# Group normalisation on one core: one load over fifteen DMA engines from the GpSimd queue in place of quarter-wise statistics and transfers

## The chip, the core and the metric

The kernel runs on one core of a Trainium2 chip. The metric is the device time of one execution in microseconds (us). Before the change it is 637.84 us, the median of three runs (637.81 to 638.18).

The core has four engines that compute: TensorE (PE in the profile, with its weight loads as PEld), VectorE (DVE), ScalarE (ACT) and GpSimd (POOL). SyncE (SP) does nothing but issue transfers here. Transfers between the memory of the chip and the core's own memory of 128 partitions are carried by sixteen DMA engines. [...]

## What is computed

```python
def reference(x, g, b):          # x: (128, 1024, 32, 16) bf16
    G = 32
    xr = x.reshape(B, G, C // G, H, W)
    mu = xr.mean(axis=(2, 3, 4), keepdims=True)
    var = ((xr - mu) ** 2).mean(axis=(2, 3, 4), keepdims=True)
    xn = (xr - mu) / jnp.sqrt(var + 1e-5)
    xn = xn.reshape(B, C, H, W)
    return xn * g[None, :, None, None] + b[None, :, None, None]
```

Each sample has 32 groups of 32 channels; a group is 32 x 512 = 16384 numbers that lie next to each other. Mean and variance are those of the group, g and b belong to the channel. 134 MB are read and 134 MB written.

## The kernel before, in words

A tile is four samples with their 32 groups each, 128 groups, one to a partition: 128 rows of 16384 bf16, 32 KB a row, 4 MB a tile. There are 32 tiles (NT) and six buffers for them (XBUFS); a result is written over its own input. All the work is unrolled. The helper `chain` keeps the instructions of one engine in the order of the program text; waits between engines come from the data. Loads and stores are all issued by SP, in one order.

For a tile i:

- `L(i)` (lines 91 to 102) loads it. Tile 0 and tile 31 go in four transfers of 1 MB (a quarter of every row), the others in one of 4 MB. The first six are issued at once. After that the load of tile i + 5 is issued behind the store of tile i, and waits for the store of tile i - 1, whose buffer it takes.
- `M(i)` (155) adds the tile up on TensorE: 32 matmuls with the identity, each taking 512 columns, 8 of them into `pa` (the first quarter of the row) and 24 into `pb`.
- `R0(i)` (189) reduces `pa` on DVE to `q`, minus the first quarter's sum over 16384. `R1(i)` (192) adds `pb` to it, which gives minus the mean, and makes the `seed`, minus the square of the distance between the quarter's mean and the whole one, in small operations (198, 210).
- `Q(i)` (221) squares the tile about its first quarter's mean on ACT, in four instructions of 4096 columns, each with a sum. The squares thus need the first quarter's sum alone.
- `V(i)` (239) makes the variance on DVE (245) with the seed as correction, its root on ACT (258), the reciprocal (266), and a scale and a bias for each channel (271, 277).
- `A(i, c)` (288) writes the result of a quarter c over the tile, a DVE instruction for each channel (305). In the last tile two channels of each quarter go to ACT (298).
- `S(i, lo, hi)` (315) stores. The last two tiles go in quarters as they are done, the others whole.

The loop runs, for every i: Q(i), M(i+1), R0(i+1), V(i), then A(i) with R1(i+1) in the middle of it, the store, and the load of tile i + 5. So on DVE the first reduction of the next tile stands ahead of V(i), and on ACT the root of tile i stands ahead of the squares of tile i + 1.

g and b are loaded once as [32, 32] each from the ACT queue, and spread to the 128 partitions by a matmul (`GB`, 141).

Of the kernel before, what the change touches and what calls it, by code (L numbers as in the profile page):

```python
# [8 lines left out]
ACT = mybir.ActivationFunctionType  # L9
ALU = mybir.AluOpType  # L10
F32 = mybir.dt.float32
BF16 = mybir.dt.bfloat16
# [8 lines left out]
QUARTERS = 4  # L21
STORE_IN_PARTS = 2
ACT_SHARE = 2
# [3 lines left out]
def kernel(  # L27
# [7 lines left out]

    nc = tc.nc
    P = nc.NUM_PARTITIONS
    B0, C, H, W = x.shape
    G = NUM_GROUPS
    HW = H * W
    assert P % G == 0 and C % G == 0
    NS = P // G
    assert B0 % NS == 0
    NT = B0 // NS
    KC = C // G  # L50
    F = KC * HW
    inv_n = 1.0 / float(F)
    MMN = MM_FREE
    NMM = F // MMN
    NQ = QUARTERS
    QF = F // NQ
    KQ = KC // NQ
    MQ = NMM // NQ
    assert NQ == 4 and F % (NQ * MMN) == 0 and KC % NQ == 0

    x_v = x.rearrange("(t n) (g k) h w -> t (n g) (k h w)", n=NS, g=G)
    o_v = out.rearrange("(t n) (g k) h w -> t (n g) (k h w)", n=NS, g=G)
# [7 lines left out]
    pspool = ctx.enter_context(  # L70
        tc.tile_pool(name="pspool", bufs=2, space=bass.MemoryType.PSUM)
    )
    gpool = ctx.enter_context(
        tc.tile_pool(name="gpool", bufs=1, space=bass.MemoryType.PSUM)
# [7 lines left out]
    def chain(key, inst):  # L82
        prev = last.get(key)
        if prev is not None:
            tc.add_manual_dep(inst.ins, prev.ins.name, nosync, reason="pipeline order")
        last[key] = inst
        return inst

    state = {}

    def L(i):
        xt = xpool.tile([P, F], BF16, name="xt")
        parts = NQ if i == 0 or i >= NT - 1 else 1
        w = F // parts
        for c in range(parts):
            chain(
                "sp",
                nc.sync.dma_start(  # L98
                    out=xt[:, c * w : (c + 1) * w], in_=x_v[i][:, c * w : (c + 1) * w]
                ),  # L100
            )
        state[i] = {"xt": xt}

    for i in range(min(UPFRONT, NT)):
        L(i)

    gb_b = consts.tile([G, 2, KC], BF16)
    chain("act", nc.scalar.dma_start(out=gb_b[:, 0, :], in_=g_v))
    chain("act", nc.scalar.dma_start(out=gb_b[:, 1, :], in_=b_v))
# [3 lines left out]
    chain("act", nc.scalar.activation(out=warm[:], in_=eps_t[:], func=ACT.Sqrt))  # L113

# [12 lines left out]
    rep = consts.tile([G, P], BF16)  # L127
    nc.gpsimd.affine_select(
        out=rep[:].rearrange("q (n a) -> q n a", n=NS),
        in_=ones_b[0:G, :].rearrange("q (n a) -> q n a", n=NS),  # L130
        pattern=[[0, NS], [-1, G]],
        compare_op=ALU.is_equal,
        fill=0.0,
        base=0,
        channel_multiplier=1,
    )
    gb = consts.tile([P, 2, KC], F32)
    gam = gb[:, 0, :]
    bet = gb[:, 1, :]

    def GB():
        gb_p = gpool.tile([P, 2, KC], F32, name="gb_p")
        chain(
            "pe",
            nc.tensor.matmul(  # L145
                out=gb_p[:].rearrange("p a k -> p (a k)"),
                lhsT=rep[:],
                rhs=gb_b[:].rearrange("q a k -> q (a k)"),
                start=True,
                stop=True,  # L150
            ),
        )
        chain("dve", nc.vector.tensor_copy(out=gb[:], in_=gb_p[:]))  # L153

    def M(i):
        st = state[i]
        for name, lo, hi in (("pa", 0, MQ), ("pb", MQ, NMM)):
            ps = pspool.tile([P, MMN], F32, name=name)
            for k in range(lo, hi):
                chain(  # L160
                    "pe",
                    nc.tensor.matmul(  # L162
                        out=ps[:],
                        lhsT=eye[:],
                        rhs=st["xt"][:, k * MMN : (k + 1) * MMN],
                        start=(k == lo),
                        stop=(k == hi - 1),
                    ),
                )
            st[name] = ps  # L170

    def sum_of(ps, seed, name):
        total = spool.tile([P, 1], F32, name=name)
        jd = jpool.tile([P, MMN], BF16, name="jd")
        chain(
            "dve",
            nc.vector.tensor_scalar(  # L177
                out=jd[:],
                in0=ps[:],
                scalar1=-inv_n,  # L180
                scalar2=seed,
                op0=ALU.mult,
                op1=ALU.add,
                accum_out=total[:],
            ),
        )
        return total

    def R0(i):
        state[i]["q"] = sum_of(state[i]["pa"], None, "q")  # L190

    def R1(i):
        st = state[i]
        st["negmean"] = sum_of(st["pb"], st["q"][:], "negmean")
        off = spool.tile([P, 1], F32, name="off")
        chain(
            "dve",
            nc.vector.tensor_scalar(  # L198
                out=off[:],
                in0=st["negmean"][:],  # L200
                scalar1=1.0 / NQ,
                scalar2=st["q"][:],
                op0=ALU.mult,
                op1=ALU.subtract,
            ),
        )
        seed = spool.tile([P, 1], F32, name="seed")
        chain(
            "dve",
            nc.vector.scalar_tensor_tensor(  # L210
                out=seed[:],
                in0=off[:],
                scalar=-1.0,
                in1=off[:],
                op0=ALU.mult,
                op1=ALU.mult,
            ),
        )
        st["seed"] = seed

    def Q(i):
        st = state[i]
        sq = spool.tile([P, NQ], F32, name="sq")
        for k in range(NQ):
            ja = jpool.tile([P, QF], BF16, name="ja")
            chain(
                "act",
                nc.scalar.activation(  # L228
                    out=ja[:],
                    in_=st["xt"][:, k * QF : (k + 1) * QF],  # L230
                    func=ACT.Square,
                    bias=st["q"][:],
                    scale=1.0 / NQ,
                    accum_out=sq[:, k : k + 1],
                ),
            )
        st["sq"] = sq

    def V(i):
        st = state[i]  # L240
        var = spool.tile([P, 1], F32, name="var")
        jv = spool.tile([P, NQ], F32, name="jv")
# [6 lines left out]
                scalar2=st["seed"][:],  # L249
# [9 lines left out]
                out=rstd[:],  # L259
                in_=var[:],  # L260
                func=ACT.Sqrt,
                bias=eps_t[:],
                scale=float(NQ * NQ),
# [8 lines left out]
                out=scl[:], in0=gam, scalar1=rstd[:], scalar2=None, op0=ALU.mult  # L272
# [8 lines left out]
                in1=bet,  # L281
# [6 lines left out]
    def A(i, c):  # L288
        st = state[i]
        xt = st["xt"]  # L290
        for k in range(c * KQ, (c + 1) * KQ):
            span = xt[:, k * HW : (k + 1) * HW]
            scl = st["scl"][:, k : k + 1]
            bia = st["bia"][:, k : k + 1]
            if i == NT - 1 and k >= (c + 1) * KQ - ACT_SHARE:
                chain(
                    "act",
                    nc.scalar.activation(  # L298
                        out=span, in_=span, func=ACT.Identity, bias=bia, scale=scl
                    ),  # L300
                )
            else:
                chain(
                    "dve",
                    nc.vector.tensor_scalar(  # L305
                        out=span,
                        in0=span,
                        scalar1=scl,
                        scalar2=bia,
                        op0=ALU.mult,  # L310
                        op1=ALU.add,
                    ),
                )

    def S(i, lo, hi):
        chain(
            "sp",
            nc.sync.dma_start(  # L318
                out=o_v[i][:, lo * QF : hi * QF],
                in_=state[i]["xt"][:, lo * QF : hi * QF],  # L320
            ),
        )

    M(0)
    R0(0)
    GB()
    R1(0)
    for i in range(NT):
        Q(i)
        if i + 1 < NT:  # L330
            M(i + 1)
            R0(i + 1)
        V(i)
        in_parts = i >= NT - STORE_IN_PARTS
        for c in range(NQ):
            A(i, c)
            if in_parts:
                S(i, c, c + 1)
            if c == NQ // 2 - 1 and i + 1 < NT:
                R1(i + 1)  # L340
        if not in_parts:
            S(i, 0, NQ)
        state.pop(i)
        j = i + AHEAD
        if UPFRONT <= j < NT:
            L(j)
# [30 lines left out]
```

## Time and profile before

| What | Value |
|---|---|
| median of three runs | 637.84 us |
| the profiled execution | 637.81 us |
| its span, first to last instruction | 636.1 us |
| moved | 268.70 MB, mean 422 GB/s over the span |
| busy: ACT, DVE, PE | 499.8, 412.6, 288.7 us |
| issue to landing, 4 MB: load, store (medians) | 29.7, 39.1 us |
| mean granted TensorE clock | 0.727 |

How to read it: the profile is of one execution, and its times start with the first instruction. A row of the timeline has start, duration, engine, line, operation, output and input, and in brackets how long the engine was idle before it and what ended that. A row of the busy windows has the window, its length, then for PE, PEld, DVE, ACT and POOL the busy time and the number of instructions, then the granted TensorE clock (1.00 is full speed), the mean busy share of the sixteen DMA engines, and what they moved in GB/s. The time that a transfer takes "to landing" runs from its issue and includes what it waits in the engines' queues behind earlier ones.

### The profile page before, as it was taken

Reading aid. Unit: us, or ns where it says so; the run is one execution under the profiler, and the core shown is the slowest. Engines: PE = TensorE matmul, PEld = TensorE weight load, DVE = VectorE, ACT = ScalarE, POOL = GpSimd, SP = SyncE. Lnnn points to the kernel's source line nnn. Section 1 sums busy time; section 2 is a strip of 40 time slices with the busy share of each in tenths; the row PEclk is TensorE's granted clock in tenths of the full one; section 3 lists DMA queues with packets and bytes.
Section 4 is the critical chain, followed back from the end, with each engine's and each line's share of the span. In section 5 each row is a group of like instructions: output and inputs, shape, how many; then the busy total and the mean of one; then the engine's idle time right before and its main releaser. Section 6 shows DMA issues by size and latency. Waiting matters only on the chain.

```text
span 636.1 us, 3995 instructions
## 1 busy us (share of the span) xinstructions
PE 288.7 (45%) x1025; PEld 113.2 (18%) x1025; DVE 412.6 (65%) x1371; ACT 499.8 (79%) x298; POOL 0.8 (0%) x6
## 2 busy tenths in 40 slices
PE   5567604563335642356433555425553445546000
PEld 2223201221112210122111222112221112212000
DVE  1388888886686665875567756677555785668740
ACT  4899999997886777977679767797767986779920
POOL 0000000000000000000000000000000000000000
PEclk9789758766788666887567875678765787668655
DMA  9999999999999999999999999999999999999993
GB/s 373 443 430 398 429 434 432 441 429 431 431 428 433 433 437 427 434 429 429 433 431 436 433 433 431 431 430 435 433 433 435 430 431 429 437 418 439 428 422 151
DMA packets 11063, 268.70 MB, mean 422 GB/s; under 512 B 1312, under 2 KB 1312, under 8 KB 1312
## 3 DMA queue, kind: packets, MB, share of 16 engines
q1 hardware_dynamic: 10944, 268.44, 98.3%
q8 instruction: 8, 0.13, 0.1%
q14 instruction: 15, 0.12, 0.0%
q10 hardware_dynamic: 96, 0.00, 0.0%
HBM read 134.22 MB, written 134.22 MB: 422 GB/s over the span
## 4 chain that ended last, share of the span: by engine, by line
DMA 80%; ACT 11%; issue 2%; DVE 2%; PE 1%; SPq 1%; DVEq 0%; ACTq 0%
DMA out_dram<-xt 72%; ACT ja L228 11%; DMA xt<-in_x_dram 8%; DVE xt L305 1%; PE pa L162 1%; SPq L98 1%; DVE jv L245 0%; ACT rstd L258 0%; DVE rstd L266 0%; DVEq L372 0%; DVE bia L277 0%; DVE scl L271 0%; DVE jd L177 0%; ACTq L228 0%; SPq L318 0%
## 5 line engine op out<-in xcount | busy, mean ns | idle before, releaser
L228 ACT ACTIVATE ja<-xt,q 128x4096 bf16<-128x4096 bf16 x128 | 474.2, 3704 | 9.9 <-DVE jd L177 6.8
L305 DVE TENSOR_SCALAR xt<-xt,scl,bia 128x512 bf16<-128x512 bf16 x1016 | 333.5, 405 | 1.2
L162 PE MATMUL pa<-xt,eye 128*128 128x512 bf16 x256 | 109.8, 607 | 298.8 <-DMA xt<-in_x_dram 298.8
L162 PEld LDWEIGHTS <-eye 128*128 128x128 bf16 x1024 | 113.1, 113 | 474.4 <-DMA xt<-in_x_dram 300.2
L162 PE MATMUL pb<-xt,eye 128*128 128x512 bf16 x768 | 184.9, 400 | 1.0 <-DMA xt<-in_x_dram 1.0
L177 DVE TENSOR_SCALAR_CACHE_REDUCE jd<-pa 128x512 bf16<-128x512 f32 x32 | 22.1, 689 | 155.8 <-PE pa L162 155.8
L258 ACT ACTIVATE rstd<-var,eps_t 128x1 f32<-128x1 f32 x32 | 9.4, 294 | 96.4 <-DVE jv L245 96.4
L228 ACT ACTIVATION_READ_ACCUMULATOR ja<-xt,q 128x1 f32 x128 | 23.9, 186 | 0.0
L177 DVE TENSOR_SCALAR_CACHE_REDUCE jd<-pb,q 128x512 bf16<-128x512 f32 x32 | 23.7, 741 | 0.0
L245 DVE TENSOR_SCALAR_CACHE_REDUCE jv<-sq,seed 128x4 f32<-128x4 f32 x32 | 6.8, 214 | 18.9 <-ACT ja L228 18.9
L266 DVE RECIPROCAL rstd<-rstd 128x1 f32<-128x1 f32 x32 | 5.2, 164 | 11.6 <-ACT rstd L258 11.6
L277 DVE SCALAR_TENSOR_TENSOR bia<-scl,negmean,gb 128x32 f32<-128x32 f32 x32 | 8.0, 251 | 1.1
L271 DVE TENSOR_SCALAR scl<-gb,rstd 128x32 f32<-128x32 f32 x32 | 7.7, 242 | 1.1
L198 DVE TENSOR_SCALAR off<-negmean,q 128x1 f32<-128x1 f32 x32 | 6.8, 214 | 1.1
L298 ACT ACTIVATE xt<-xt,bia,scl 128x512 bf16<-128x512 bf16 x8 | 5.8, 800 | 0.8 <-DVE bia L277 0.8
L210 DVE SCALAR_TENSOR_TENSOR seed<-off 128x1 f32<-128x1 f32 x32 | 5.1, 159 | 1.1
L153 DVE COPY gb<-gb_p 128x64 f32<-128x64 f32 x1 | 0.2, 225 | 5.3 <-PE gb_p L145 5.3
L245 DVE DVE_READ_ACCUMULATOR jv<-sq,seed 128x1 f32 x32 | 2.6, 83 | 0.0
L177 DVE DVE_READ_ACCUMULATOR jd<-pa 128x1 f32 x32 | 2.6, 82 | 0.0
L113 ACT ACT_TABLE_LOAD x1 | 1.3, 1283 | 1.7 <-PEq L361 1.7
L177 DVE DVE_READ_ACCUMULATOR jd<-pb,q 128x1 f32 x32 | 2.5, 80 | 0.0
L111 DVE MEMSET eps_t<- 128x1 f32 x1 | 0.1, 59 | 0.9 <-PEq L361 0.9
(10 smaller groups left out, 1.7 us busy)
## 6 DMA issues: line engine op xcount, KB each, us to landing
xt<-in_x_dram SPq DMA_DIRECT2D x30, 4096.0 KB, 29.7
out_dram<-xt SPq DMA_DIRECT2D x30, 4096.0 KB, 39.1
xt<-in_x_dram SPq DMA_DIRECT2D x8, 1024.0 KB, 16.8
out_dram<-xt SPq DMA_DIRECT2D x8, 1024.0 KB, 25.3
gb_b<-in_g_dram ACTq DMA_DIRECT2D x1, 2.0 KB, 3.3
gb_b<-in_b_dram ACTq DMA_DIRECT2D x1, 2.0 KB, 5.3
```

The lines of the kernel that those rows point to most:

```text
L98: nc.sync.dma_start(out=xt[:, c * w : (c + 1) * w], in_=x_v[i][:, c * w : (c + 1) * w]),
L162: nc.tensor.matmul(out=ps[:], lhsT=eye[:], rhs=st["xt"][:, k * MMN : (k + 1) * MMN], start=(k == lo), stop=(k == hi - 1),),
L177: nc.vector.tensor_scalar(out=jd[:], in0=ps[:], scalar1=-inv_n, scalar2=seed, op0=ALU.mult, op1=ALU.add, accum_out=total[:],),
L198: nc.vector.tensor_scalar(out=off[:], in0=st["negmean"][:], scalar1=1.0 / NQ, scalar2=st["q"][:], op0=ALU.mult, op1=ALU.subtract,),
L228: nc.scalar.activation(out=ja[:], in_=st["xt"][:, k * QF : (k + 1) * QF], func=ACT.Square, bias=st["q"][:], scale=1.0 / NQ, accum_out=sq[: ...
L245: nc.vector.tensor_scalar(out=jv[:], in0=st["sq"][:], scalar1=inv_n, scalar2=st["seed"][:], op0=ALU.mult, op1=ALU.add, accum_out=var[:],),
L258: nc.scalar.activation(out=rstd[:], in_=var[:], func=ACT.Sqrt, bias=eps_t[:], scale=float(NQ * NQ),),
L266: chain("dve", nc.vector.reciprocal(out=rstd[:], in_=rstd[:]))
L271: nc.vector.tensor_scalar(out=scl[:], in0=gam, scalar1=rstd[:], scalar2=None, op0=ALU.mult),
L277: nc.vector.scalar_tensor_tensor(out=bia[:], in0=scl[:], scalar=st["negmean"][:], in1=bet, op0=ALU.mult, op1=ALU.add,),
L298: nc.scalar.activation(out=span, in_=span, func=ACT.Identity, bias=bia, scale=scl),
L305: nc.vector.tensor_scalar(out=span, in0=span, scalar1=scl, scalar2=bia, op0=ALU.mult, op1=ALU.add,),
```

## The change

The diff replaces one set of edits by another. Out go the quarters: the first quarter's statistics, the split load of tiles 0 and 31, the stores of the last two tiles in parts, and ACT's share in writing the last tile. Squares are taken about the whole mean, which needs the sum over all 32 matmuls; `R0` and `R1` become one reduction `R`. g and b are loaded four times each to fill 128 partitions, and the matmul that spread them goes.

In comes a load that is split by rows. Tile 16's rows 0 to 119 are loaded by one transfer from the GpSimd queue, its rows 120 to 127 by one from SP. The limit on the length of a row's piece (`max_dma_last_dim`) is given as 16384. Two tiny transfers from the GpSimd queue, of 4 and 13 partitions, stand before and behind; 4 + 15 + 13 = 32, twice the number of engines. The change is described as a load over fifteen engines which leaves out engine 3.

```diff
+SQ_FREE = 4096
+SPLIT_TILE = 16
+WIDE = 120
...
+    def turn(n):
+        t = tpool.tile([n, 4, 4], BF16, name=f"turn{n}")
+        chain("pool", nc.gpsimd.dma_start(
+                out=t[:, :, 0:2],
+                in_=g[0 : n * 8].rearrange("(p a c) -> p a c", a=4, c=2)))
+
     def L(i):
         xt = xpool.tile([P, F], BF16, name="xt")
-        parts = NQ if i == 0 or i >= NT - 1 else 1
...
+        if i == SPLIT_TILE:
+            chain("pool", nc.gpsimd.dma_start(
+                    out=xt[0:WIDE, :], in_=x_v[i][0:WIDE, :], max_dma_last_dim=F))
+            chain("sp", nc.sync.dma_start(out=xt[WIDE:P, :], in_=x_v[i][WIDE:P, :]))
+            turn(32 - 4 - 15)
+        else:
+            chain("sp", nc.sync.dma_start(out=xt[:], in_=x_v[i]))
...
     for i in range(min(UPFRONT, NT)):
         L(i)
+    turn(4)
...
+    for n in range(NS):
+        chain("act", nc.scalar.dma_start(out=gam_b[n * G : (n + 1) * G, :], in_=g_v))
+        chain("act", nc.scalar.dma_start(out=bet_b[n * G : (n + 1) * G, :], in_=b_v))
...
     def M(i):
-        for name, lo, hi in (("pa", 0, MQ), ("pb", MQ, NMM)):
+        ps = pspool.tile([P, MMN], F32, name="ps")
+        for k in range(NMM):
...
     def Q(i):
-                    bias=st["q"][:],
-                    scale=1.0 / NQ,
+                    bias=st["negmean"][:],
+                    scale=1.0,
...
     def V(i):
-                scalar2=st["seed"][:],
+                scalar2=None,
...
-    def A(i, c):
-            if i == NT - 1 and k >= (c + 1) * KQ - ACT_SHARE:
+    def A(i):
+        for k in range(KC):
...
     M(0)
-    R0(0)
-    GB()
-    R1(0)
+    R(0)
     for i in range(NT):
         Q(i)
         if i + 1 < NT:
             M(i + 1)
-            R0(i + 1)
+            R(i + 1)
         V(i)
-        in_parts = i >= NT - STORE_IN_PARTS
...
+        A(i)
+        S(i)
         j = i + AHEAD
         if UPFRONT <= j < NT:
             L(j)
```

The sums now go into one tile `ps` with three buffers in place of two for each of `pa` and `pb`.

## The prediction, made before the changed kernel was run

> **What bounds the kernel now.** I read the page's slices, queues and chain first, then busy windows over the last 14 us, then the timeline of the last two tiles.
>
> ```profile
> DMA  9999999999999999999999999999999999999993
> q1 hardware_dynamic: 10944, 268.44, 98.3%
> q8 instruction: 8, 0.13, 0.1%
> DMA 80%; ACT 11%; issue 2%; DVE 2%; PE 1%; SPq 1%; DVEq 0%; ACTq 0%
> ```
>
> ```profile
> 112.00:560.00 448.00, 212.63 (x736) 82.60 (x736) 300.83 (x1000) 356.84 (x210) 0.00 (x0) 0.72 1.00 432
> ```
>
> The transfers bound it: no slice but the last is below 9, and from 112 to 560 us (last two columns of the window row) the sixteen DMA engines are fully busy at 432 GB/s. ACT, the busiest compute engine, works 356.84 of those 448 us. At 432 GB/s a tile of 4.19 MB takes 4.19/432 = 9.71 us, so one of an engine's eight rows takes 1.21 us. 64 such transfers are 621 us, yet the span is 636.1. The rest is in the tail.
>
> ```profile
> 622.00:623.00 1.00, 0.00 (x0) 0.00 (x0) 0.00 (x0) 0.00 (x0) 0.00 (x0) 0.50 0.95 401
> 624.00:625.00 1.00, 0.00 (x0) 0.00 (x0) 0.00 (x0) 0.00 (x0) 0.00 (x0) 0.50 0.72 303
> 626.00:627.00 1.00, 0.00 (x0) 0.00 (x0) 0.00 (x0) 0.00 (x0) 0.00 (x0) 0.50 0.25 107
> 628.00:629.00 1.00, 0.00 (x0) 0.00 (x0) 0.00 (x0) 0.00 (x0) 0.00 (x0) 0.50 0.12 49
> 630.00:631.00 1.00, 0.00 (x0) 0.00 (x0) 0.00 (x0) 0.00 (x0) 0.00 (x0) 0.50 0.06 25
> 634.00:635.00 1.00, 0.00 (x0) 0.00 (x0) 0.00 (x0) 0.00 (x0) 0.00 (x0) 0.50 0.04 16
> ```
>
> A share of 0.06 is 1/16. So most engines have run dry by 625, four work in 626 to 627 (0.25), two at 628 (0.12), and from about 629 to 634.7 a single one. One engine is some 6 us behind the second slowest and 9 us behind the middle. Its lag is not a wait at the end but work that piled up: queue q8 alone carries 8 instruction blocks of 16 KB, and 0.1% of 16 engines' 636.1 us is about 10 us of one engine (5 to 15 by rounding). The views don't number the engines.
>
> The lag reaches the compute too, since a load has landed only when its slowest engine has:
>
> ```profile
> 566.08 3.20 PE L162 MATMUL pa<-xt,eye 128*128 128x512 bf16 x8 [9.84 <-DMA xt<-in_x_dram]
> 569.32 0.69 DVE L177 TENSOR_SCALAR_CACHE_REDUCE jd<-pa 128x512 bf16<-128x512 f32 x1 [5.47 <-PE pa L162]
> 570.39 3.69 ACT L228 ACTIVATE ja<-xt,q 128x4096 bf16<-128x4096 bf16 x1
> ...
> 579.19 3.47 PE L162 MATMUL pa<-xt,eye 128*128 128x512 bf16 x8 [4.73 <-DMA xt<-in_x_dram]
> 586.17 3.69 ACT L228 ACTIVATE ja<-xt,q 128x4096 bf16<-128x4096 bf16 x1
> 586.64 1.89 PE L162 MATMUL pb<-xt,eye 128*128 128x512 bf16 x8 [0.53 <-DMA xt<-in_x_dram]
> 601.49 0.22 DVE L245 TENSOR_SCALAR_CACHE_REDUCE jv<-sq,seed 128x4 f32<-128x4 f32 x1 [2.90 <-ACT ja L228]
> 602.84 7.83 DVE L305 TENSOR_SCALAR xt<-xt,scl,bia 128x512 bf16<-128x512 bf16 x24
> ```
>
> The first quarter of tile 31 has landed at 579.19, its last at 586.64. After that load come five whole stores (tiles 27 to 31): 586.6 + 5 x 9.71 = 635.2, which is where the slow engine ends. So it never paused; subtracting 6 us, the second slowest has tile 31 at about 580.8.
>
> **The change, part by part.** *Relief.* Tile 16's load goes as 120 rows over fifteen engines, eight each, and 8 rows from SP. The engine left out is spared 8 rows and takes back one of the 8 SP rows if they are spread one to an engine: 7 x 1.21 = 8.5 us. That exceeds the 6 us by which the worst engine trails the second, so, if it is the one left out, the second governs. The second itself gets 0 rows or 1 row more (0 to 1.2 us); I take half, 0.6. Tile 31 then lands at 580.8 + 0.6 = 581.4 (bounds 580.8 to 582.0).
>
> *Small transfers.* g and b go in eight transfers of 48 packets (32 rows and 16 completions) in place of two: 384 packets for 96. The row of q10 shows 0.0% for 96, so under 0.05% of 16 x 636.1, 5.1 us, under 53 ns each: at most 288 x 53/16 = 1.0 us per engine. The two tiny transfers have 16 and 52 pieces, at most 0.3 us per engine by the same row. Twelve fewer big transfers give a little back. I take 0.3 for all, and 0 to 1.3 for the range.
>
> *GpSimd's issue* has no row; the nearest are SP's 0.34 us and GpSimd's own selection of 0.29 us. It waits for tile 10's store to land, with only the second tiny transfer behind it on its queue; SP waits for the same store, as it does now, with tile 12's store behind it. Cover: SP's rings then still hold tile 15's load and tile 11's store, 19.4 us less the lag of at most 9, so 10 us of issue cost nothing; a load takes 29.7 us to land today. Beyond that, each us is lost. I take 0, bounds 0 to 1. A gain is excluded, since the bytes are the same.
>
> *Statistics.* Each tile loses a second reduction (0.74 + 0.08 us) and two small operations (0.21 + 0.16), 1.2 us of DVE; DVE is 65% busy, so this is worth nothing in the middle. But the squares now wait for the whole tile's sum: 32 matmuls, 3.47 us for the first eight and 5.34 for the next 24, so 8.8 instead of 3.5.
>
> *Start.* Tile 0 is whole only at 13.1 (the third group of pb starts at 13.14), so sums end at 22.0, squares run 23.0 to 38.3, and with 1.35 us for the scales and 32 x 0.326 = 10.4 us of writing, the store issues at 50.1 rather than 39.86. The rings are busy with six loads until about 61, so nothing is lost. Tile 1's store follows 15.8 later, at 66, needed by 61 + 9.7 = 70.7. The cover is 4.7 us; the price is one for one beyond it. I take 0.
>
> *Tail.* Here the removed parts were at work. Tile 31: lands 581.4, +0.3 for the small transfers; sums to 590.5; from the last matmul to the first square 1.1 (569.28 to 570.39): 591.6; squares 15.3 (586.17 to 601.46): 606.9; 1.35 to the first write (601.49 to 602.84), 608.3; all 32 writes on DVE at 7.83/24 = 0.326 each, 10.4: 618.7. ACT's help is gone (2.6 us) and the store goes whole. Issue to landing without a queue: the first quarter took 0.80 to 5.71, 4.9 us, of which 2.4 is data, so 2.5 of overhead; 618.7 + 2.5 + 9.7 = 630.9. The other limit is the second slowest engine's ring: 628.9 + 0.6 + 0.3 = 629.8. Both agree within about 1 us. Tile 30's store, held by tile 31's sum on DVE, issues at about 603; the rings run dry without it near 605. From the last packet at 634.7 to the span's end the old run needs 1.4, of which about 0.5 lies in my landing overhead: I add 0.9.
>
> *Sum.* 631.8 against 636.1, -4.3 us. The profiled execution took 637.81, the lowest of the three, whose median is 637.84; so 633.5. I put it at 633.3, because the ring limit lies a little below.
>
> [...] The trace shows one engine late by 6 us but not which. [...]
>
> **The rivals.**
> - *The late engine isn't relieved* (another is left out, or the late one isn't engine 3). For it: no row before numbers an engine. Against: the 8.5 us spared are just the size of the 9 us lag. Tile 31 then lands at 586.6 to 587.9, and the same 37.3 us of chain, 2.5 + 9.7 and 0.9 follow: 637.0 to 638.3, +0.9 to +2.2, so 638.7 to 640.0, in the middle 639.4: slower. The removal of quarters and parts is then unpaid. It decides from a landing at about 587.0, where the time passes 639.1.
> - *The tensor clock stays low through tile 31's sums.* The first eight take 0.43 us each, the next 24 0.22, in every stage shown. If all 32 took 0.43, the sums need 13.9, 5.1 more, all on the chain: 638.4, no change. Against: the clock rose after eight in every tile.
> - *The start starves the rings.* If tile 0's sums take those 5.1 us more, tile 1's store comes 0.4 after its 70.7; with an ACT delay of another 3 us it costs 3.4: 636.7, still faster. Slight.
> - *The compute tail is hidden*: tile 31 lands earlier, near 579, because fast engines are not gated. Then the ring limit alone: about 632.
>
> **How the numbers follow.** Relief as described: 0.70, 631 to 636, predicted 633.3. Not relieved: 0.20. Low clock: 0.06. Starved start: 0.04. The relieved case's own range is 631.0 to 636.0: 633.3 less 2.3 for a landing at 580, nothing for the small transfers and the ring limit, plus 2.7 for the far ends of relief, small transfers and issue. The whole range runs to 640.0, to take in the unrelieved case. What a measurement can tell from no change is 0.2%, 1.3 us, so 636.6 to 639.1. Faster: 0.67 of the relieved case and 0.03 of the starved start, 0.70. Same: 0.06 of the low clock, 0.03 from the relieved case's upper end and 0.03 of the unrelieved, 0.12. Slower: the rest, 0.18.
>
> **What would show it.** In the changed profile: the single-engine tail at 0.06 is gone; the sums of tile 31 wait for its load until about 581.5; tile 31's last square ends near 607 and the last write near 619; the share dips between about 616 and 620, while the last store is being made, then is full to 630. A landing at 587 and a lone engine beyond 635 would show the first rival; slices below 9 before 620 a starved ring.

## The result and the profile after

The changed kernel takes 646.56 us in the median of four runs (645.80 to 646.60); the kernel before, on the same chip, 638.01 us (637.81 to 638.27). The ratio is 1.0131, with a 95% interval of 1.0113 to 1.0149: the change costs 8.6 us. I had forecast 633.3, so the sign was wrong as well as the size. The profiled execution took 645.80 us with a span of 644.1, against 637.81 and 636.1 before.

First the page's slices (40 of 16.1 us each) and its queues:

```profile
DMA  9999699999999999999999999999999999999986
GB/s 371 440 424 427 294 391 422 426 440 429 424 430 435 424 429 442 417 374 391 438 434 428 434 431 438 426 437 431 429 434 431 430 438 428 433 435 433 429 360 277
...
q1 hardware_dynamic: 9088, 264.51, 96.1%
q0 software_dynamic: 336, 3.93, 1.7%
q8 instruction: 8, 0.13, 0.1%
...
q10 hardware_dynamic: 384, 0.02, 0.0%
```

Two dents are new. The fifth slice falls to 6 in the busy digits and to 294 GB/s: for a part of it the engines had nothing to do. (A slice below 9 before 620 us was the sign that I had given for a starved ring.) The 18th and 19th move 374 and 391 GB/s while the digit stays at 9: the engines were busy, but slower. The queues hold what the change announces: q0 now carries 3.93 MB, the 120 rows, and q10 has 384 packets in place of 96.

The first dent, closer, by busy windows. The second dent follows in the same view:

```profile
62.00:72.00 10.00, 7.08 (x32) 3.05 (x32) 7.85 (x27) 9.70 (x8) 0.00 (x0) 1.00 0.86 368
72.00:82.00 10.00, 0.00 (x0) 0.00 (x0) 6.13 (x23) 9.73 (x6) 0.00 (x0) 0.50 0.61 262
82.00:92.00 10.00, 0.00 (x0) 0.00 (x0) 9.72 (x31) 9.90 (x7) 0.00 (x0) 0.50 1.05 413
92.00:102.00 10.00, 3.86 (x10) 1.39 (x11) 6.40 (x23) 9.74 (x6) 0.00 (x0) 0.50 0.95 374
...
272.00:282.00 10.00, 0.00 (x0) 0.00 (x0) 7.97 (x25) 9.90 (x7) 0.00 (x0) 0.50 0.97 355
282.00:292.00 10.00, 8.61 (x32) 3.50 (x32) 0.00 (x0) 1.95 (x2) 0.00 (x0) 0.74 1.03 377
292.00:302.00 10.00, 0.30 (x2) 0.00 (x0) 9.20 (x32) 8.79 (x6) 0.00 (x0) 0.77 0.99 400
```

Against the 432 GB/s of the long middle, the first four windows move (4 x 432 - 368 - 262 - 413 - 374) x 10 / 432 = 7.2 us too little, with shares down to 0.61. The last three move 3.8 us too little by the same sum, with shares of 0.97 to 1.03.

Why the engines ran dry at 70 us is read from the timeline of the start:

```profile
3.94 0.46 ACTq L122 DMA_DIRECT2D gam_b<-in_g_dram  x1
13.07 0.32 ACTq L123 DMA_DIRECT2D bet_b<-in_b_dram  x1
13.10 9.21 PE L148 MATMUL ps<-xt,eye 128*128 128x512 bf16 x32 [13.10 <-DMA xt<-in_x_dram]
...
28.20 0.18 DVE L139 CAST gam<-gam_b 128x32 f32<-128x32 bf16 x1 [27.09 <-DMA gam_b<-in_g_dram]
31.81 0.18 DVE L140 CAST bet<-bet_b 128x32 f32<-128x32 bf16 x1 [3.43 <-DMA bet_b<-in_b_dram]
31.90 0.68 DVE L164 TENSOR_SCALAR_CACHE_REDUCE jd<-ps 128x512 bf16<-128x512 f32 x1
32.63 3.71 ACT L183 ACTIVATE ja<-xt,negmean 128x4096 bf16<-128x4096 bf16 x1 [30.32 <-DVE jd L164]
...
59.71 16.06 SPq L256 DMA_DIRECT2D out_dram<-xt  x2
...
594.94 8.44 PE L148 MATMUL ps<-xt,eye 128*128 128x512 bf16 x32 [9.79 <-DMA xt<-in_x_dram]
619.75 0.16 DVE L200 TENSOR_SCALAR_CACHE_REDUCE jv<-sq 128x4 f32<-128x4 f32 x1 [4.00 <-ACT ja L183]
621.04 10.43 DVE L245 TENSOR_SCALAR xt<-xt,scl,bia 128x512 bf16<-128x512 bf16 x32
```

Tile 0 has landed at 13.10 and its sums are done at 22.3, as forecast. But two copies stand ahead of the first reduction on VectorE, of gamma and of beta to float32, at 28.20 and 31.81. They wait for loads of 2 KB each, issued from the ACT queue (the first two rows are the last load of gamma and the last of beta), and beta's lands just before 31.81. The reduction, ready for 9.6 us, starts at 31.90, the squares at 32.63, and the first store is issued at 59.71. The line of that store counts two issues over 16.06 us, so the second came at about 75.4; the rings were to have had it by 70.7. Tile 31 lands at 594.94 rather than 581.7, and from there the chain runs as forecast: 49.2 us to the end of the span at 644.1 (50.1 forecast).

### The profile page after: what moved, and what is told of

Read it like the earlier page. It is cut to its first block, busy times and chain, and to the rows that moved or that the text cites. A ratio compares the mean times of both kernels' runs of the same rounds, so it can differ in the third digit from the quotient of the medians.

```text
span 644.1 us, 3825 instructions
## 1 busy us (share of the span) xinstructions
PE 283.4 (44%) x1024; PEld 111.9 (17%) x1024; DVE 380.1 (59%) x1252; ACT 494.1 (77%) x290; POOL 2.6 (0%) x8
## 3 DMA queue, kind: packets, MB, share of 16 engines
q0 software_dynamic: 336, 3.93, 1.7%
## 4 chain that ended last, share of the span: by engine, by line
DMA 60%; ACT 19%; PE 8%; another core or an unknown queue 5%; DVE 4%; issue 1%; SPq 0%; DVEq 0%
DMA xt<-in_x_dram 29%; DMA out_dram<-xt 28%; ACT ja L183 19%; PE ps L148 8%; DVE xt L245 3%; DMA bet_b<-in_b_dram 3%; DVE jd L164 1%; DVE jv L200 0%; ACT rstd L213 0%; DVE scl L222 0%; DVE bia L228 0%; DVE rstd L217 0%; SPq L107 0%; DVEq L297 0%
## 5 line engine op out<-in xcount | busy, mean ns | idle before, releaser
L183 ACT ACTIVATE ja<-xt,negmean 128x4096 bf16<-128x4096 bf16 x128 | 474.2, 3704 | 33.4 <-DVE jd L164 30.3
L148 PE MATMUL ps<-xt,eye 128*128 128x512 bf16 x1024 | 283.4, 446 | 320.0 <-DMA xt<-in_x_dram 320.0
L164 DVE TENSOR_SCALAR_CACHE_REDUCE jd<-ps 128x512 bf16<-128x512 f32 x32 | 22.0, 688 | 157.4 <-PE ps L148 157.3
L200 DVE TENSOR_SCALAR_CACHE_REDUCE jv<-sq 128x4 f32<-128x4 f32 x32 | 4.9, 154 | 47.6 <-ACT ja L183 47.6
L183 ACT ACTIVATION_READ_ACCUMULATOR ja<-xt,negmean 128x1 f32 x128 | 23.8, 186 | 0.0
L228 DVE SCALAR_TENSOR_TENSOR bia<-scl,negmean,bet 128x32 f32<-128x32 f32 x32 | 8.0, 251 | 1.1
L222 DVE TENSOR_SCALAR scl<-gam,rstd 128x32 f32<-128x32 f32 x32 | 7.7, 241 | 1.1
L200 DVE DVE_READ_ACCUMULATOR jv<-sq 128x1 f32 x32 | 2.6, 83 | 0.0
L164 DVE DVE_READ_ACCUMULATOR jd<-ps 128x1 f32 x32 | 2.6, 82 | 0.0
L87 POOL DMA_DIRECT2D turn_85<-in_g_dram x1 | 0.7, 712 | 0.9 <-POOLq L286 0.9
L87 POOL DMA_DIRECT2D turn_1224<-in_g_dram x1 | 0.6, 566 | 0.0
```

Of the source, the lines that this page charges most:

```text
L87: nc.gpsimd.dma_start(out=t[:, :, 0:2], in_=g[0 : n * 8].rearrange("(p a c) -> p a c", a=4, c=2),),
L148: nc.tensor.matmul(out=ps[:], lhsT=eye[:], rhs=st["xt"][:, k * MMN : (k + 1) * MMN], start=(k == 0), stop=(k == NMM - 1),),
L164: nc.vector.tensor_scalar(out=jd[:], in0=st["ps"][:], scalar1=-inv_n, scalar2=None, op0=ALU.mult, op1=ALU.add, accum_out=negmean[:],),
L183: nc.scalar.activation(out=ja[:], in_=st["xt"][:, k * SQ_FREE : (k + 1) * SQ_FREE], func=ACT.Square, bias=st["negmean"][:], scale=1.0, acc ...
L200: nc.vector.tensor_scalar(out=jv[:], in0=st["sq"][:], scalar1=inv_n, scalar2=None, op0=ALU.mult, op1=ALU.add, accum_out=var[:],),
L222: nc.vector.tensor_scalar(out=scl[:], in0=gam[:], scalar1=rstd[:], scalar2=None, op0=ALU.mult),
```

## The experiments

Two questions were put: how much of the loss is the start and how much the split load, and by what mechanism each arises. Every kernel below computes the whole of the reference. Each ratio is to the kernel before, run on the same chip at the same time. That kernel took 638.38 to 638.57 us on the chips of the experiments and 638.01 on that of the change, so differences of medians between chips hold to about half a us. A trace shows one execution, and some of these kernels scatter (the next one from 638.49 to 642.29 us); where the traced execution lies over 1 us off the median, the text says so.

**The copies behind the reduction.** From the changed kernel, the two copies move behind tile 0's reduction on VectorE:

```diff
-    nc.vector.tensor_copy(out=gam[:], in_=gam_b[:])
-    nc.vector.tensor_copy(out=bet[:], in_=bet_b[:])
...
     R(0)
+    chain("dve", nc.vector.tensor_copy(out=gam[:], in_=gam_b[:]))
+    chain("dve", nc.vector.tensor_copy(out=bet[:], in_=bet_b[:]))
```

> The changed kernel with the two copies of gamma and beta on DVE behind the first reduction instead of ahead of it. Theory A (the first reduction stands behind the copy of beta, which waits until 31.8 us for a 2 KB load whose packets alternate with 32 KB ones; the squares start 9.6 us late and the DMA engines run dry between 71 and 92 us): squares start at about 23 us, the first store issues at about 50, no window from 62 to 102 us moves under 400 GB/s, and about 7 of the 8.5 us come back: 639.5 us, 638.5 to 640.7. Theory B (the late start is absorbed by the buffers, all of the loss is tile 16's load): 645 to 646.6 us.

Measured: 640.22 us, ratio 1.0022 (1.0009 to 1.0034), 6.3 us less than the change. The timeline of this kernel's start, and the row of tile 31's sums (the traced execution took 638.49 us, the fastest of ten):

```profile
22.68 0.69 DVE L162 TENSOR_SCALAR_CACHE_REDUCE jd<-ps 128x512 bf16<-128x512 f32 x1 [21.57 <-PE ps L146]
23.41 3.71 ACT L181 ACTIVATE ja<-xt,negmean 128x4096 bf16<-128x4096 bf16 x1 [21.11 <-DVE jd L162]
28.79 0.18 DVE L259 CAST gam<-gam_b 128x32 f32<-128x32 bf16 x1 [5.41 <-DMA gam_b<-in_g_dram]
...
50.49 16.06 SPq L254 DMA_DIRECT2D out_dram<-xt  x2
...
587.55 9.02 PE L146 MATMUL ps<-xt,eye 128*128 128x512 bf16 x32 [11.24 <-DMA xt<-in_x_dram]
```

The reduction now waits for the sums alone, and the store is issued at 50.49, where the prediction had 50.1. From 72 to 82 us the windows show 419 GB/s in place of 262. The small loads are as late as ever (gamma is copied at 28.79), but nobody waits for them before the first scales at about 39.

**The load over sixteen engines.** From the changed kernel, tile 16 goes like every other tile and both tiny transfers go:

```diff
-SPLIT_TILE = 16
+SPLIT_TILE = -1
...
-    turn(4)
```

> The changed kernel with tile 16 loaded like the others from SP, and without the two tiny transfers. Theory A (GpSimd's load costs every engine about 4 us, because packets of two queues take turns and each gets longer, and gives the one late engine its 8.5 us; the next late engine then governs): the median engine lands tile 31 some 4 us earlier but the slowest about as now, 593.6 against 594.9: 645.2 us, 644 to 646.5. Theory B (the load is a plain loss): 642.5 us. Theory C (the relief works as predicted and only the start was wrong): 650 us or more.

Measured: 643.45 us, 1.0076 (1.0056 to 1.0096), 3.1 us less than the change. So the split load with its relief made the changed kernel slower, not faster.

**Both undone together**, the two edits above in one kernel:

> The changed kernel with both: copies behind the first reduction, and tile 16 from SP. Theory A (the quarters, the parts and ACT's share, whose loss is left, are worth nothing as long as one DMA engine is 9 us late): 638.0 us, 637.2 to 639.2, with a single engine at a share of 0.06 at the end as in the kernel before. Theory B (they were worth some us of their own in the tail): 640 us or more.

Measured: 636.88 us, 0.9977 (0.9967 to 0.9986). The two parts add up: 6.3 + 3.1 = 9.4 against 646.56 - 636.88 = 9.7. And this version is faster than both kernels, by 1.6 us than the one before. It has neither quarters nor parts nor ACT's share, and no relief. Its timeline at the end (the traced execution took 635.75 us, the fastest of ten):

```profile
584.93 8.48 PE L145 MATMUL ps<-xt,eye 128*128 128x512 bf16 x32 [11.93 <-DMA xt<-in_x_dram]
...
611.07 10.42 DVE L242 TENSOR_SCALAR xt<-xt,scl,bia 128x512 bf16<-128x512 bf16 x32
```

Its tile 31 lands at 584.93, where the kernel before had its last quarter at 586.64; from there to its span's end at 634.0 it takes 49.1 us. With the split load and its relief put back, which is the kernel with the copies moved, tile 31 lands at 587.55: later, not earlier.

**Where the packets of the small loads wait.** From the changed kernel with the copies left ahead of the reduction, tile 0 comes in four quarters, so that its rows are pieces of 8 KB rather than 32:

```diff
-            chain("sp", nc.sync.dma_start(out=xt[:], in_=x_v[i]))
+            parts = 4 if i == 0 else 1
+            w = F // parts
+            for c in range(parts):
+                chain("sp", nc.sync.dma_start(
+                    out=xt[:, c * w : (c + 1) * w],
+                    in_=x_v[i][:, c * w : (c + 1) * w]))
```

> The changed kernel with tile 0's load in four quarters as in the kernel before, the copies left ahead of the first reduction. Theory A (the small loads of gamma and beta take turns with the packets of the tile loads, one for one, so 24 packets an engine wait 24 x 1.21 us among 32 KB packets and far less among 8 KB ones): beta has landed by about 12 us, squares start near 23, and the time is that of the run with the copies moved, 639.5 to 641 us. Theory B (what holds beta is that its last transfer is issued only at 13 us): 644.5 to 646.6 us.

Measured: 640.1 us, 1.0025 (1.0007 to 1.0043), the same as with the copies moved. The timeline (the traced execution took 638.87 us):

```profile
9.33 0.18 DVE L149 CAST bet<-bet_b 128x32 f32<-128x32 bf16 x1
...
16.23 0.69 DVE L173 TENSOR_SCALAR_CACHE_REDUCE jd<-ps 128x512 bf16<-128x512 f32 x1 [6.71 <-PE ps L157]
16.96 3.71 ACT L192 ACTIVATE ja<-xt,negmean 128x4096 bf16<-128x4096 bf16 x1 [14.66 <-DVE jd L173]
```

The same eight small loads are all in by 9.33 us. What made them late was the size of the pieces beside them: beta's copy starts at 31.81 us beside pieces of 32 KB. Here the last load of beta is also issued earlier, at 6.17 us in place of 13.07, so this run alone doesn't rule out Theory B. The changed kernel's own rows do: gamma's last load, issued at 3.94, was copied only at 28.20, and beta's came 3.6 us behind it, which is three times 1.21 us. So beta was not held by its late issue alone: gamma's last load, issued early, took 24.1 us to land. The 384 packets of q10 are 24 for each of sixteen engines if they are spread evenly; if each waits for one 32 KB row of 1.21 us (an eighth of a tile's 9.71 us, by estimate), that is an estimate of 29 us, and the changed kernel copied beta at 31.81. With 8 KB rows the same estimate gives 7.3 us, and gamma's and beta's copies start at 9.1 and 9.3. No view shows in what order an engine takes its packets, so turns of one for one remain an estimate, which fits both kernels.

**The split load alone**, put into the kernel before, with the same two tiny transfers:

```diff
+        if i == SPLIT_TILE:
+            chain("pool", nc.gpsimd.dma_start(
+                out=xt[0:WIDE, :], in_=x_v[i][0:WIDE, :], max_dma_last_dim=F))
+            chain("sp", nc.sync.dma_start(out=xt[WIDE:P, :], in_=x_v[i][WIDE:P, :]))
+            turn(32 - 4 - 15)
...
+    turn(4)
```

> The kernel before with nothing but tile 16's load over fifteen engines from GpSimd and the two tiny transfers. Theory A (4 us of lengthened packets on every engine, and another engine that is 8 us late after it): 638 to 640 us, no gain. Theory B (the relief works as predicted, the second slowest engine governs at about 629): 632 to 634 us.

Measured: 638.62 us, 1.0004 (0.9995 to 1.0013). No gain, and Theory A's range was met.

**Another engine meant to be left out**: the kernel of the run above with 9 and 8 partitions in the tiny transfers in place of 4 and 13. It was meant to leave out engine 8 and not engine 3; no view here numbers an engine, so which one is left out is not shown:

```diff
-            turn(32 - 4 - 15)
+            turn(8)
...
-    turn(4)
+    turn(9)
```

> [...] Theory A (engine 3 is the late one, it was relieved in that run, and its relief was paid for with some 3.4 us on every engine): the late engine keeps its lag and the cost comes on top: 640.5 to 642.5 us, with a single engine at 0.06 for more than 6 us at the end. Theory B (it doesn't matter which engine is left out): 638 to 639.5 us as there.

Measured: 643.09 us, 1.0071 (1.0056 to 1.0086). So 643.09 - 638.62 = 4.5 us hang on the two tiny transfers. Had the 120 rows fallen to the same engines in both kernels, tile 16 would be loaded alike; the 4.5 us speak for rows that fall to other engines when the tiny transfers change, which is an inference. That engine 3 was the late one and was relieved would fit it: here the split costs 643.09 - 638.38 = 4.7 us, so that in the split load alone cost and relief would cancel. It isn't shown: if the rows of tile 16 fall to other engines, the split itself may cost the engines differently too.

The windows of the last microseconds, first of the split load alone, then of the kernel with 9 and 8 partitions:

```profile
628.00:630.00 2.00, 0.00 (x0) 0.00 (x0) 0.00 (x0) 0.00 (x0) 0.00 (x0) 0.50 0.42 176
632.00:634.00 2.00, 0.00 (x0) 0.00 (x0) 0.00 (x0) 0.00 (x0) 0.00 (x0) 0.50 0.07 29
634.00:636.00 2.00, 0.00 (x0) 0.00 (x0) 0.00 (x0) 0.00 (x0) 0.00 (x0) 0.50 0.06 25
```

```profile
628.00:630.00 2.00, 0.00 (x0) 0.00 (x0) 0.00 (x0) 0.00 (x0) 0.00 (x0) 0.50 0.46 193
636.00:638.00 2.00, 0.00 (x0) 0.00 (x0) 0.00 (x0) 0.00 (x0) 0.00 (x0) 0.50 0.12 49
638.00:640.00 2.00, 0.00 (x0) 0.00 (x0) 0.00 (x0) 0.00 (x0) 0.00 (x0) 0.50 0.06 25
640.00:642.00 2.00, 0.00 (x0) 0.00 (x0) 0.00 (x0) 0.00 (x0) 0.00 (x0) 0.50 0.03 12
```

From 628 to 630 the mean share has fallen below a half alike in both kernels (0.42 and 0.46), so the difference lies in the last engines and not in all of them. And even in the split load alone, a lone engine (0.06) works at the end, to about 636. The views don't number it: it may be another engine that grew late, or the late one, never relieved.

**The GpSimd queue without the split.** What slows the split load? My first theory was the second queue: that GpSimd's packets and SP's hold each other up. In the kernel before, tile 16 goes whole, 128 rows, from GpSimd:

```diff
+        if i == 16:
+            nc.gpsimd.dma_start(out=xt[:], in_=x_v[i], max_dma_last_dim=F)
+            state[i] = {"xt": xt}
+            return
```

> The kernel before with tile 16's whole load, 128 rows over all sixteen engines, from GpSimd in pieces of 16 KB; nobody is relieved. Theory A (turns between two queues lengthen the packets of both, 3.4 us on every engine): 641 to 642 us. Theory B (the second queue costs nothing and the loss lies in the uneven split): 638 to 639 us.

Measured: 639.0 us, 1.0010 (1.0001 to 1.0019): 0.6 us. This theory fell. What was left was the split by rows.

**The split without the GpSimd queue.** In the kernel before, tile 16 goes in two transfers by rows, both from SP, as 120 + 8 and as 112 + 16; the second has counts that divide by sixteen:

```diff
+        if i == 16:
+            chain("sp", nc.sync.dma_start(out=xt[0:120, :], in_=x_v[i][0:120, :]))
+            chain("sp", nc.sync.dma_start(out=xt[120:P, :], in_=x_v[i][120:P, :]))
+            state[i] = {"xt": xt}
+            return
```

> The kernel before with tile 16's load as 120 rows and 8 rows, both from SP; GpSimd has no part in it. Theory A (the loss of the fifteen-way load lies in its split: with 120 rows the engines no longer keep to the rows, and so to the partitions, that each has to itself in a 128-row transfer, and they get in each other's way): between 262 and 312 us fewer than 420 GB/s are moved, and the time is 639.5 to 642 us. Theory B (it takes GpSimd's queue beside SP's): 430 GB/s there, and 638 to 639.3 us.

> The kernel before with tile 16's load as 112 rows (seven to each of sixteen engines) and 16 rows (one to each), both from SP. [...] Theory A (the partitions matter, not the number of engines): fewer than 425 GB/s between 262 and 312 us and 639 to 641 us. Theory A2 (an uneven number of engines matters): 430 GB/s and 638 to 639 us.

Measured: 120 + 8 takes 650.89 us, 1.0197 (1.0180 to 1.0214), 12.5 more than before; 112 + 16 takes 646.14 us, 1.0119 (1.0104 to 1.0134), 7.7 more. Both cost more than Theory A allowed for. Cutting one load by rows, as 120 + 8, costs more than the whole change did (8.6).

**Two controls**, with the same lines but the cut elsewhere: by columns (two transfers of 128 rows and half a row's length), and by rows into 64 + 64 (64 in place of 120 in the first two lines):

```diff
-            chain("sp", nc.sync.dma_start(out=xt[0:120, :], in_=x_v[i][0:120, :]))
-            chain("sp", nc.sync.dma_start(out=xt[120:P, :], in_=x_v[i][120:P, :]))
+            h = F // 2
+            chain("sp", nc.sync.dma_start(out=xt[:, 0:h], in_=x_v[i][:, 0:h]))
+            chain("sp", nc.sync.dma_start(out=xt[:, h:F], in_=x_v[i][:, h:F]))
```

> The kernel before, with tile 16 loaded by two SP transfers of 128 rows and half a row's length each. Theory A (what costs is that the rows of a transfer fall to the engines otherwise than in a transfer of 128 rows): nothing changes here, 638.4 us (638.0 to 639.5), and 262 to 312 us move 425 to 432 GB/s. Theory B (a second transfer for a tile in mid-stream costs, however it is cut): 642 or more, under 410 GB/s. Theory C (an uneven number of rows or of engines costs: 120 is fifteen engines, 112 is seven rows of each): 638.4 as with A.

> The kernel before, with tile 16 loaded by two SP transfers of 64 whole rows each, so four rows to each of the sixteen engines, twice. Theory A: an engine gets other rows than in a transfer of 128, so time is lost, at least as much as with 112 rows and 16: 646 us or more (643 at the least), and 262 to 312 us move 360 GB/s or less. Theory B: 642 or more, the same as the cut by columns. Theory C: the counts are even, so 638.4 us and 425 to 432 GB/s.

Measured: the cut by columns takes 638.19 us, 0.9993 (0.9984 to 1.0003), no change; 64 + 64 takes 645.71 us, 1.0114 (1.0099 to 1.0129), 7.1 more. The windows from 262 to 312 us, one line for each kernel, in this order: before; whole from GpSimd; cut by columns; the split of the change in the kernel before; 64 + 64; 112 + 16; 120 + 8:

```profile
262.00:312.00 50.00, 20.36 (x68) 7.91 (x69) 32.37 (x107) 40.10 (x24) 0.00 (x0) 0.70 1.00 431
```

```profile
262.00:312.00 50.00, 18.95 (x64) 7.35 (x66) 32.00 (x107) 36.90 (x22) 0.85 (x1) 0.69 1.00 425
```

```profile
262.00:312.00 50.00, 20.16 (x68) 7.77 (x69) 32.75 (x108) 40.38 (x24) 0.00 (x0) 0.71 1.00 432
```

```profile
262.00:312.00 50.00, 18.93 (x64) 7.24 (x64) 29.39 (x99) 34.28 (x21) 1.34 (x2) 0.67 1.01 409
```

```profile
262.00:312.00 50.00, 18.13 (x65) 7.01 (x64) 30.09 (x101) 34.99 (x21) 0.00 (x0) 0.73 1.00 351
```

```profile
262.00:312.00 50.00, 19.03 (x63) 7.28 (x64) 29.30 (x99) 34.20 (x21) 0.00 (x0) 0.68 1.00 355
```

```profile
262.00:312.00 50.00, 16.40 (x54) 6.44 (x56) 23.32 (x79) 28.20 (x17) 0.00 (x0) 0.66 1.00 326
```

The share is 1.00 or 1.01 in every line, and the rate goes from 432 down to 326 GB/s. The three that keep each transfer at 128 rows keep the rate (425 to 432 GB/s), whatever the queue and however many transfers; all those cut by rows lose it, even 64 + 64 with its even counts. So it is neither a second transfer nor a count that doesn't divide by sixteen that costs by itself, but the cut by rows. That it costs because the engines get other rows than a transfer of 128 gives them is the reading that is left; no view shows which rows an engine gets. At worst, the 120 + 8 kernel moves this (same columns):

```profile
282.00:286.00 4.00, 0.00 (x0) 0.00 (x0) 3.93 (x14) 3.97 (x3) 0.00 (x0) 0.99 0.96 238
286.00:290.00 4.00, 0.00 (x0) 0.00 (x0) 2.75 (x9) 3.97 (x3) 0.00 (x0) 0.50 0.92 188
```

That is down to less than half of the usual rate, with engines over nine tenths busy. What slows them no view shows. If the engines get other rows, they write to other partitions and read other parts of x, and no run tells the two apart.

**The relief put at the very end.** In the kernel before, the second half of tile 31's store goes as 120 rows from GpSimd and 8 from SP, between the same tiny transfers, so that no load behind it could lose anything:

```diff
+            nc.gpsimd.dma_start(
+                out=o_v[i][0:120, a:z], in_=state[i]["xt"][0:120, a:z],
+                max_dma_last_dim=z - a)
+            nc.sync.dma_start(
+                out=o_v[i][120:P, a:z], in_=state[i]["xt"][120:P, a:z])
```

> The kernel before with relief at the end: the second half of tile 31's store goes as 120 rows over fifteen engines from GpSimd and 8 rows from SP. Theory A (relief helps where it comes last and little is left to take turns with): the late engine is spared 7 half rows, 4.2 us, the others lose 1 to 2: 634 to 636 us. Theory B (the turns cost as much as the relief gives, as in the middle): 638 to 639.5 us.

Measured: 638.39 us, 0.9999 (0.9990 to 1.0008). No gain. The windows near its end:

```profile
619.00:621.00 2.00, 0.00 (x0) 0.00 (x0) 0.00 (x0) 0.00 (x0) 0.00 (x0) 0.50 0.93 324
621.00:623.00 2.00, 0.00 (x0) 0.00 (x0) 0.00 (x0) 0.00 (x0) 0.00 (x0) 0.50 1.08 356
623.00:625.00 2.00, 0.00 (x0) 0.00 (x0) 0.00 (x0) 0.00 (x0) 0.00 (x0) 0.50 0.94 311
```

The store split by rows shows the same mark, full shares at 311 to 356 GB/s. Theory B's time came. But in its last microseconds, 634 to 635, a lone engine works at a share of 0.04, just as in the kernel before. Whether relief was won here and paid for in the same place, or the late engine wasn't the one left out, these views don't tell.

## Why the prediction was wrong

By medians, 646.56 - 633.3 = 13.3 us lie between time and forecast. They divide so (each step on top of the one above it; the last compares two chips and is 0.5 us larger if each kernel is taken against the kernel before on its own chip):

| step | forecast | measured | difference, us |
|---|---|---|---|
| the tail's parts removed, nothing relieved (first rival's middle) | 639.4 | 636.88, both undone | -2.5 |
| split load and relief on top | -6.1 | +3.3 (640.22 - 636.88) | +9.4 |
| the start on top | 0 | +6.3 (646.56 - 640.22) | +6.3 |

Three terms of the sum failed; they stand here in the order of time. The smaller part, 6.3 us, is the start, and its cause is shown. The larger, 9.4 us, is the split load and its relief, and there a part stays open.

**The first step that failed** is *Start*: "The rings are busy with six loads until about 61, so nothing is lost. Tile 1's store follows 15.8 later, at 66, needed by 61 + 9.7 = 70.7. The cover is 4.7 us; the price is one for one beyond it. I take 0." The cover was about right and the price a little low: with everything 9.6 us late, the second store came at 75.4, 4.7 us after it was needed, and the time lost was 6.3. What failed is the 50.1. I derived it from tile 0's sums alone and left out the two copies that the diff puts ahead of the reduction on the same engine, because under *Small transfers* I had costed the eight loads by the busy time of their packets (0.3 us). That price was of the wrong kind: it is when they land that decides, by 31.8 us beside 32 KB rows against 9.33 us beside 8 KB ones. The removed quarters had kept tile 0's pieces at 8 KB. The third of my rivals, a start that starves the rings, named this outcome, but by a slow tensor clock, with 0.04 and 636.7; the clock was granted at 1.00 from 12 to 32 us.

**The second step that failed** is *GpSimd's issue*: "I take 0, bounds 0 to 1. A gain is excluded, since the bytes are the same." The issue from GpSimd cost little (0.6 us for the whole load). But equal bytes didn't mean equal time: the windows lose 3.8 us in the changed kernel, and the run with tiny transfers of 9 and 8 partitions loses 4.7. I had bounded the issue and never asked for a bound on the transfer's own rate; every row of the trace that I priced by was a transfer of 128 rows.

**The third step that failed** is *Relief*. Tile 31's landing was to go from 586.6 to 581.4, 5.2 us earlier. Between the two kernels that differ in the split load alone it went from 584.93 to 587.55. Relief and split together cost 3.3 us where I had forecast a gain of 6.1, and with the split's 3.8 to 4.7 us taken off, relief is left with a gain of 0.5 to 1.4 us: 4.7 to 5.6 us of it didn't come. Two things are known. The unrelieved form lands tile 31 at 584.93 already, so less was to be won; and with the split load a lone engine still ends last (a share of 0.06). Why tile 31 comes earlier there is open, and so is whether engine 3 was the late one: the 4.5 us between the two pairs of tiny transfers speak for it, the lone engine that is left speaks against it. No run shows which engine is left out, nor the eight rows to an engine that the 8.5 us rest on; in their place the runs show the 0.5 to 1.4 us. My reason for the lag, the instruction blocks of queue q8, was varied by no run.

**The first rival** had the late engine unrelieved and the parts at the tail unpaid, at 639.4. The parts were worth nothing: without them, and without relief, the kernel takes 636.88. That the kernel with the copies moved takes 640.22, close to 639.4, is luck: the parts came out 2.5 us cheaper and the split, which the rival didn't price, 3.3 dearer. The sums, squares and writes of tile 31 add up as worked out (8.5, 15.3 and 10.4 us); it was the landing I took too late by 1.7 to 3.0 us (586.6 to 587.9 against 584.93, in an execution 1.1 us faster than the median).

*Statistics*, the cost of squares about the whole mean in the middle, was rightly 0: with both other parts undone the 262 to 312 us windows move 433 GB/s. *Tail* was right from landing to end within 1 us. The second rival, a clock that stays low through tile 31's sums, didn't come: they took 8.44 us where 8.8 was reckoned. That the clock rose after eight matmuls in every tile, the argument against it, goes too far: in the kernel before the first eight took 3.20 to 3.60 us in 30 of 32 tiles and 1.90 us in tiles 2 and 4, and tile 0's took 3.48 us at a granted clock of 1.00.

## What to carry to other kernels

A small load is priced by when it lands, not by its bytes (here by 9.33 us beside 8 KB pieces and by 31.8 us beside 32 KB ones): look at the size of the pieces that are under way beside it and at what the program puts behind its consumer on the same engine, and put that consumer behind work which doesn't need it. Where the DMA engines are the bound, keep every large transfer at all 128 partitions and cut it by columns, not by rows; a cut by rows of one load among 64 transfers cost 7.1 to 12.5 us here when all came from SP, and a cut by columns nothing (638.19 us against 638.57). Take the price of a transfer from a row of its own shape, and where there is none, measure it alone before building on it.

## What the runs showed of the hardware that was not expected

A load of 128 rows cut into two by rows took the engines to as little as 188 GB/s at a share of 0.92, while the same load cut by columns, or sent whole from GpSimd beside SP's ring, stayed at 432 and 425 GB/s. The three cuts from SP cost 12.5 us (120 + 8), 7.7 (112 + 16) and 7.1 (64 + 64); the same 120 + 8 with its larger part from GpSimd cost only 4.7 with tiny transfers of 9 and 8 partitions, and 0.1 with 4 and 13 (638.62 against 638.51). Why GpSimd's is the cheaper is open; in the changed kernel its pieces are also half as long, 16 KB (q0's 3.93 MB are 240 packets of 8 KB or more, for 120 rows).

Eight transfers of 2 KB (384 packets in the changed kernel) were all in by 9.33 us beside 8 KB pieces, and beside 32 KB pieces only at 31.8 us.
